# Turning keys and queries head by head into natural order, with one evacuation a bank

## The chip, the cores and the metric

One Trainium2 chip, one of its cores. The metric is the device time of one execution in microseconds (us), the median of several runs. Five engines work side by side, each through its own instruction list in order: TensorE (PE; its weight loads are shown as PEld), VectorE (DVE), ScalarE (ACT), GpSimd (POOL) and SyncE (SP), which issues nearly all DMAs.

## The reference, cut to what matters

Three stages in a row, on a batch of 2, 768 positions, 8 heads of 64 (512 channels):

```python
k_sum = k.reshape(B, H, nb, 32, D).max(axis=3)      # maxima of blocks of 32 keys
v_sum = v.reshape(B, H, nb, 32, D).mean(axis=3)
scores = concat([where(|i-j| < 16, q @ k.T / 8, -1e9), q @ k_sum.T / 8 + log(32)])
x  = softmax(scores) @ concat([v, v_sum])            # heads side by side: (2, 768, 512)
h  = relu(x @ w_in);  x2 = (h * sigmoid(conv3(h)) @ w_out)     # 512 -> 1024 -> 512
out = x2 + relu(layernorm(x2) * g @ w_ch1) @ w_ch2   # 512 -> 2048 -> 512
```

The weights come as float64 and are narrowed to float32 on the chip.

## The kernel before, in words

Work is cut into some 1,850 pieces ("ops" of a plan). Each has a name, the engines it may run on, and the pieces it must follow; the string ORDER lists all of them, each with the letter of the engine it runs on (P, V, A, G, S). The list is fixed in the file, and each engine's instructions stand in the order of the list. A piece that waits therefore holds up all later pieces of its engine.

**Attention.** The 1,536 positions are 6 chunks of 256 (0 to 2 are batch 0, 3 to 5 batch 1). Keys of a chunk become `kw`, queries `qb`: the 64 channels of a head lie on partitions, even heads on partitions 0 to 63, odd heads on 64 to 127, four heads each along the free axis, then positions. To get there, rows from HBM are turned by TensorE into a PSUM bank of 128x512 (`transposed`, L342, two banks a chunk; pieces `kt`, `kb`, `qt`) and the bank is evacuated to SBUF (`ke`, `kn`, `qe`). There are two layouts of a load. In a "pair" load (L324, keys 0 to 2 and all queries) a partition holds positions 2p and 2p+1 of every head, so that a piece of HBM is 512 B. A transposed bank then has the even positions on its lower 64 partitions and the odd ones on its upper 64, and the evacuation is two instructions of 64x512 that write every second position (L413, L801). In a natural load (L879, keys 3 to 5) a partition is one position, a piece of HBM is 256 B, two heads make one transposed block, and the evacuation is one instruction of 128x512 (L377). Block maxima (`km`, L810) are taken of `kw` for chunks 0 to 2, one instruction of 128x1024 a chunk, and of the bank (`kmb`, L369), one of 128x512 a bank, for 3 to 5. Copies of keys at the edges of 64-position windows (`kh`, `kx`) and of the maxima (`kc`) complete `kw`.

A pair of windows j (0 to 11) then goes: mask and scores on PE (`M`, `S`; L462, L470), maximum on DVE (`X`, L523), exponential on ACT (`E`, L535), sum and its inverse on DVE (`Q`, `R`), normalisation (`N`, L554, POOL or DVE), transpose on PE (`P`, L564), evacuation (`C`, ACT or DVE, tile probT), product with values (`T`, L486), and the split into a high and a low part (`H` on ACT or DVE, `L` on DVE, L508). Values come by `lv` (SP, L599, 256 B pieces); block means of values of batch 0 by matmuls on a pair load (`vb`, L826), of batch 1 by DVE reductions (`vr`, L944).

**Middle layers.** 48 steps i (6 chunks of positions by 8 blocks of 128 hidden channels): `h` (12 matmuls, L701), relu on ACT (L713), three taps (`b` on any engine; two DVE instructions, L729), tanh on ACT, gate on DVE (`g`, L742), high part on ACT (`u`, L753), low part on POOL (`v`, L760), and `x`, 2 x 3 matmuls into the output (L773). Weights come by `lw` into six staging places and are narrowed by DVE, ACT, DVE, ACT, POOL in turn (`wi`, `wo`: L621, L625, L630, L640, L642). The `wo` tiles lie where the early loads of keys, queries and values were, and wait for those to be turned.

**Last layers.** Per batch: layer-norm statistics, normalisation, 32 DVE block transposes in two halves (`lr`, L1076), scaled high and low parts (`la` ACT, `lz` DVE, L1085). Then 32 rounds of `ch` (two halves of 12 matmuls, L1106), high and low part (`ca` ACT, `cv` DVE), and `ac` (six of 3 matmuls, L1141). Their weights (`lwy`, pieces `y`) go the same way as `w`.

The lines at issue in the old turning and evacuation of queries are

```python
T.transpose(pt[:, i * 128:(i + 1) * 128], t[:, (2 * i + hf) * 128:(2 * i + hf + 1) * 128], ident)   # L353
for r in range(2):                                                                                  # L415
    scaled(e, qb[n % 2][s, :, :, r:64:2], pts[key][64 * r:64 * r + 64].rearrange(...), SCALE)
```

Of the kernel before, what the change touches and what calls it, by code (L numbers as in the profile page):

```python
# [3 lines left out]
2G 0V 8S 6V 12S 11S 13S 58S 1P 3G 175G 225G 4G 10S 49V 154G 50A 51V 5G 9S 64S 33P 31P 34A 76S 32V 26P 24P 27A 14S 7G  # L4
157P 35V 158P 43P 25A 36V 15S 59V 60A 28V 29G 16S 44A 18P 61V 20P 37V 19A 70S 41P 21V 52P 42A 17S 22V 23G 78A 77V
88S 62A 65V 56P 38A 79V 63G 54P 66A 30V 159P 82S 55A 45P 67V 155S 80A 57V 68A 81G 39A 46P 40A 160V 72A 69G 94S 167V
161A 71V 47P 73V 100S 168A 162V 163V 164V 53V 89V 178S 48A 165P 169V 170V 171G 181P 180P 166V 90A 182P 84A 156V 172P
74A 91V 179S 373S 173A 83V 75G 190V 92A 174P 377S 183V 85V 93G 184A 106S 95V 191A 200S 185V 186V 187V 101V 96A 207P
192V 193V 188P 176A 205S 194G 177V 208P 209P 86A 189A 97V 87G 195P 102A 210V 211A 206S 217V 229S 196V 212V 197P 218A
213V 103V 214G 198V 398S 230P 108A 231P 219V 232P 220V 107V 98A 221G 109V 104A 99G 222P 240V 215P 110A 233V 223A  # L10
199V 241A 105G 112S 201P 378V 111G 234A 118S 216V 124S 202A 399P 235V 236V 400P 374V 203P 237G 224P 393S 204A 421G
238P 242V 243V 375S 379S 226A 401P 244G 239V 227V 114A 422S 245P 113V 409V 246A 228V 120A 402V 250P 410A 119V 251P
115V 252P 121V 247P 116A 411V 412V 413V 253A 117G 254A 263P 248V 403A 394P 255V 264P 665G 130S 265P 256V 122A 423P
666S 424P 404V 266A 405V 425P 406V 123G 257A 267A 249V 126A 276P 426V 277P 395A 268V 278P 136S 269V 414P 258V 279A
407P 125V 259A 289P 127V 270A 260G 132A 290P 433V 291P 415A 131V 261P 292A 408V 293A 280G 262P 271V 427A 281V 302P
# [12 lines left out]
698V 517A 536P 677A 518G 720P 537A 505G 549P 728V 538G 550P 686G 539V 551P 525V 506P 540V 552A 526V 541A 685P 527V
721V 528A 740S 699P 687V 722A 562P 529V 507P 688V 530A 519P 723V 724V 542V 725V 520P 543A 531G 563P 564P 544G 532P
565A 566V 553G 533P 567V 568V 545P 554V 569A 546V 726P 575P 727A 555V 576P 700A 570V 577P 556A 547P 578A 557V 558A  # L30
706P 548V 571A 588P 559G 729A 1130V 589P 572G 560P 1128V 1129V 590P 730V 731V 707V 732G 561P 591A 1131V 592A 579V
741P 742P 593V 743P 580V 581V 601P 744V 582A 573P 751V 745A 602P 583V 603P 594V 712P 604A 746V 747V 733P 584A 748G
605V 614P 595A 752A 615P 585G 734V 574P 606V 616P 607V 869P 713V 608A 586P 617A 868P 587P 753V 754V 609V 870P 596V
755V 597A 610A 627P 598G 878V 735P 871V 611G 879A 890G 756P 749P 891S 757V 628P 872A 629P 880V 881V 882V 599P 630A
873V 874V 875V 892P 640P 631G 618A 619V 641P 642P 620V 632V 736G 893P 621A 600P 622V 643A 633V 612P 623A 737V 634A
624G 613P 738V 625P 644V 635V 708P 645V 636A 646V 637G 647A 750V 867S 626P 709A 648V 894P 710V 649A 650G 739V 758P
902V 895V 876P 759A 761P 877V 896A 762P 760V 763P 883P 764A 897V 898V 638P 899V 884A 765G 774P 903A 766V 775P 767V
776P 768A 639P 904V 905V 777A 906G 769V 778A 651P 653P 779V 652A 780V 770A 900P 654V 781A 907P 771G 901A 787P 1132V
908A 788P 1134V 789P 782V 772P 790A 1135V 1133V 1136V 783A 1137G 791V 800P 773P 801P 784G 792V 802P 785P 793V 803A
# [65 lines left out]
ALU = mybir.AluOpType  # L105
AX = mybir.AxisListType
# [54 lines left out]
def local_summary_attention_moe_kernel(  # L161
# [180 lines left out]
    def transposed(nm, n, hf, ring):  # L342
# [908 lines left out]
```

## Time and profile before

| | us |
|---|---|
| median of 3 runs | 510.57 (509.83 to 513.29) |
| the profiled execution | 509.58 |
| its span | 507.8 |
| PE busy in the span | 481.0 (95%) |
| DVE / ACT / POOL busy | 320.0 / 232.6 / 138.5 (63 / 46 / 27%) |
| mean granted TensorE clock | 0.99 |

The span is cut into 40 slices of 12.7 us on the profile's page; the attention and the narrowing of weights fill the first five, the middle layers run from about 50 to 240 us with the rest of the attention between them, and the last layers from about 212 us to the end.

### The profile page before, as it was taken

What the parts mean: (1) busy time and instruction counts of PE and PEld (TensorE: products, weight loads), DVE (VectorE), ACT (ScalarE), POOL (GpSimd) and SP (SyncE); (2) the same over time, 40 slices, a digit from 0 to 9 for tenths busy, and PEclk for the clock granted to TensorE, in tenths of its full rate; (3) what the DMA queues carried; (4) which work ended last, traced back from release to release, by engine and by line L of the source; (5) the groups of instructions that cost most, each with busy time, mean ns of one, the idle gap of its engine ahead of it and who ended that gap; (6) DMA issues with size and microseconds to landing.
All of it is one profiled execution on the core that took longest, in us unless ns stands there. A gap on an engine that the chain in (4) does not pass through costs nothing.

```text
span 507.8 us, 8440 instructions
## 1 busy us (share of the span) xinstructions
PE 481.0 (95%) x3222; PEld 414.9 (82%) x3222; DVE 320.0 (63%) x624; ACT 232.6 (46%) x607; POOL 138.5 (27%) x166
## 2 busy tenths in 40 slices
PE   6777899999999989999999999999999999999996
PEld 4355788888888877778898899988999899999995
DVE  4989899988897799999999933241443112221113
ACT  5988788776656565555554512242233011011110
POOL 4456455533323333315433201132224000000000
PEclk9889999999999999999999999999999999999999
DMA  8999957201020130002442500252220000200003
GB/s 271 344 260 277 197 143 170 70 1 33 18 45 1 38 131 0 1 1 85 163 159 92 166 1 1 83 166 83 84 83 1 0 1 1 105 21 1 0 1 125
DMA packets 56096, 43.44 MB, mean 86 GB/s; under 512 B 26092, under 2 KB 50952, under 8 KB 56056
## 3 DMA queue, kind: packets, MB, share of 16 engines
q1 hardware_dynamic: 55912, 42.78, 29.4%
q8 instruction: 25, 0.41, 0.4%
q14 instruction: 15, 0.12, 0.1%
q10 hardware_dynamic: 144, 0.13, 0.1%
HBM read 39.22 MB, written 3.15 MB: 83 GB/s over the span
## 4 chain that ended last, share of the span: by engine, by line
PE 64%; DVE 16%; issue 6%; DMA 5%; ACT 4%; POOL 2%; SPq 2%; DVEq 0%; POOLq 0%; ACTq 0%
PE acc L1141 22%; PE ch L1106 22%; PE h L701 7%; PE x L773 6%; DVE c L729 5%; DVE xf L1076 3%; POOL wl L642 2%; DMA raw<-in_moe_w_ch_dram 2%; PE sc L470 2%; DMA wst<-in_moe_w_out_dram 1%; DMA early<-in_q_dram 1%; DVE g L742 1%; PE tr L564 1%; PE av L486 1%; DVE parts L944 1%
## 5 line engine op out<-in xcount | busy, mean ns | idle before, releaser
L1141 PE MATMUL acc<-wh,ch 128*128 128x512 f32 x382 | 126.8, 395 | 0.7 <-DVE ch L1117 0.7
L1117 DVE SCALAR_TENSOR_TENSOR ch<-ch,ch 128x384 fp32r<-128x384 f32 x64 | 35.2, 555 | 127.9 <-ACT ch L1113 127.6
L1113 ACT ACTIVATE ch<-ch 128x384 fp32r<-128x384 f32 x64 | 30.9, 492 | 161.8 <-PE ch L1106 89.9
L1106 PE MATMUL ch<-xnT,wh 128*128 128x384 f32 x512 | 99.9, 337 | 0.0
L1106 PEld LDWEIGHTS ch<-xnT,wh 128*128 128x128 f32 x512 | 90.7, 188 | 4.7 <-DVE ch L1117 0.7
L701 PE MATMUL h<-xT,wi 128*128 128x258 f32 x576 | 83.8, 290 | 7.2 <-ACT h L713 6.9
L701 PEld LDWEIGHTS h<-xT,wi 128*128 128x128 f32 x576 | 74.8, 189 | 16.3 <-ACT h L713 12.3
L1141 PEld LDWEIGHTS acc<-wh,ch 128*128 128x128 f32 x382 | 71.5, 188 | 16.3 <-DVE ch L1117 1.5
L1141 PE MATMUL acc<-wl,ch 128*128 128x512 f32 x191 | 75.1, 393 | 0.0
L642 POOL TENSOR_TENSOR wl<-raw,wh 128x512 fp32r<-128x512 f32 x32 | 43.6, 1374 | 108.6 <-ACT wh L640 77.5
L760 POOL TENSOR_TENSOR glo<-g,ghi 128x256 fp32r<-128x256 f32 x48 | 39.9, 837 | 84.4 <-ACT ghi L753 77.5
L773 PE MATMUL x<-wo,ghi 128*128 128x512 f32 x192 | 61.6, 401 | 0.2 <-ACT ghi L753 0.2
L729 DVE SCALAR_TENSOR_TENSOR c<-h,ccol,c 128x256 f32<-128x256 f32 x96 | 53.5, 568 | 5.3 <-ACT c L251 3.2
L1106 PE MATMUL ch<-xnT,wl 128*128 128x384 f32 x256 | 54.9, 336 | 0.0
L1106 PEld LDWEIGHTS ch<-xnT,wl 128*128 128x128 f32 x256 | 45.4, 188 | 0.0
L1141 PEld LDWEIGHTS acc<-wl,ch 128*128 128x128 f32 x191 | 35.8, 188 | 6.6
L773 PE MATMUL x<-wo,glo 128*128 128x512 f32 x96 | 38.0, 396 | 0.1
L1076 DVE STREAM_TRANSPOSE xf<-xn 32x384 f32<-32x384 f32 x64 | 36.5, 570 | 1.4
L773 PEld LDWEIGHTS x<-wo,ghi 128*128 128x128 f32 x192 | 32.3, 189 | 4.7 <-ACT ghi L753 0.7
L535 ACT ACTIVATE prob<-sc,nm 128x120 f32<-128x120 f32 x96 | 33.2, 367 | 1.9 <-DVE nm L523 1.4
L734 ACT ACTIVATE c<-c 128x256 f32<-128x256 f32 x48 | 20.1, 419 | 23.5 <-DVE c L729 23.1
L640 ACT CAST wh<-raw 128x512 fp32r<-128x512 f32 x32 | 20.7, 659 | 14.8 <-DVE raw L630 12.6
(130 smaller groups left out, 584.0 us busy)
## 6 DMA issues: line engine op xcount, KB each, us to landing
raw<-in_moe_w_ch_dram SPq DMA_DIRECT2D x32, 512.0 KB, 5.2
wst<-in_moe_w_out_dram SPq DMA_DIRECT2D x8, 512.0 KB, 6.0
vw<-in_v_dram SPq DMA_DIRECT2D x20, 192.0 KB, 4.2
wst<-in_moe_w_in_dram SPq DMA_DIRECT2D x5, 512.0 KB, 7.9
s_q<-in_q_dram SPq DMA_DIRECT2D x4, 512.0 KB, 7.0
early<-in_k_dram SPq DMA_DIRECT2D x3, 512.0 KB, 5.1
x2a<-in_moe_w_in_dram SPq DMA_DIRECT2D x3, 512.0 KB
early<-in_v_dram SPq DMA_DIRECT2D x3, 512.0 KB, 7.2
```

Of the source, the lines that this page charges most:

```text
L535: A.activation(out=pr[:, p, :], in_=sc[:, p * NK:(p + 1) * NK], func=AF.Exp, bias=nm[:, p:p + 1], scale=1.0, accum_out=sm[:, p:p + 1])
L640: d = plan.op(name + "d", (("A", 520),), lambda e: A.copy(hi(), narrowed(raw())), [c_] + list(extra))
L642: lambda e: G.tensor_tensor(out=lo(), in0=narrowed(raw()), in1=hi().bitcast(F32), op=ALU.subtract),
L701: T.matmul(live["h", i][:, 0:CH + 2], w_[:, c, f * 128:(f + 1) * 128], x_[:, c, :], start=(k_ == 0 and c == 0), stop=(k_ == 2 and c == 3))
L729: V.scalar_tensor_tensor(out=ct, in0=ht[:, kk:kk + CH], scalar=ccol[:, kk * NF + f:kk * NF + f + 1], in1=ct, op0=ALU.mult, op1=ALU.add)
L760: on[e].tensor_tensor(out=glo, in0=live.pop(("g", i)), in1=live["ghi", i].bitcast(F32), op=ALU.subtract)
L773: T.matmul(x2ps[g, t], l[:, ts_], r[:, f, :], start=(f == 0 and j == 0), stop=(f == NF - 1 and j == 2))
L1076: V.transpose(out=o_, in_=i_)
L1106: T.matmul(cp[:, 0:384], w_[:, c * 128:(c + 1) * 128], x_[:, c, s], start=(n_ == 0), stop=(n_ == 11))
L1113: A.activation(out=chs[b, m][0][:, s], in_=live[key][:, 0:384], func=AF.Relu)
L1117: V.scalar_tensor_tensor(out=lo[:, s], in0=live.pop(key)[:, 0:384], scalar=0.0, in1=hi[:, s].bitcast(F32), op0=ALU.max, op1=ALU.subtract)
L1141: T.matmul(acc[key], l[:, ts_], r[:, 512:1024], start=(mm == 0 and j == 0), stop=(done and j == 2))
```

## The change

For keys 0 to 2 and queries 0 and 1 the load stays a pair load, but a bank is now made by eight plain matmuls instead of four transposes: the data (one head, one parity of positions: 128x64) is the stationary operand, the identity (128x128) the moving one, the result goes to 64 partitions and to every second column. Even heads land on the lower half and odd heads on the upper half, positions in natural order. Queries 2 to 5 get a natural load (two DMAs of 256 KB in 256 B pieces instead of one of 512 KB in 512 B pieces) and the four transposes that keys 3 to 5 had. All evacuations of keys and queries are one instruction of 128x512. Block maxima of keys 0 to 2 are read from the bank, six instructions of 128x512 instead of three of 128x1024.

```diff
-        if nm == "k" and n >= NCH:
+        if n >= (NCH if nm == "k" else 2):
             tv = t.rearrange("p (r h e) -> p r h e", h=4, r=2)
...
         else:
-            for i in range(4):
-                T.transpose(pt[:, i * 128:(i + 1) * 128], t[:, (2 * i + hf) * 128:(2 * i + hf + 1) * 128], ident)
+            tv = t.rearrange("p (h a e d) -> p h a e d", h=4, a=2, e=2)
+            ov = pt.rearrange("p (h j e) -> p h e j", h=2, e=2)
+            for i in range(2):
+                for e in range(2):
+                    for a in range(2):
+                        T.matmul(ov[64 * a:64 * a + 64, i, e, :], tv[:, 2 * hf + i, a, e, :], ident,
+                                 start=True, stop=True)
...
-                s = slice(64 * pp, 64 * pp + 64)
-                for r in range(2):
-                    scaled(e, qb[n % 2][s, :, :, r:64:2],
-                           pts[key][64 * r:64 * r + 64].rearrange("p (h w j) -> p h w j", h=4, w=NW), SCALE)
-            es = [plan.op(f"qe{n}{pp}", (("A", 956), ("V", 1196)), f,
+                scaled(e, qb[n % 2][:, 2 * pp:2 * pp + 2], pts[key].rearrange("p (h w j) -> p h w j", h=2, w=NW), SCALE)
+            es = [plan.op(f"qe{n}{pp}", EVAC, f,
...
-            e_ = plan.op(f"ke{n}{hh}", (("A", 956), ("V", 1196)), f, [t])
+            e_ = k_evac(n, hh, t, [])
+            KE[n].append(e_)
+            KM[n] = KM.get(n, []) + [kmax_op(n, hh, t, key)]
             e_.give.append((r_, key))
-            KE[n].append(e_)
+            KM[n][-1].give.append((r_, key))
...
+    def q_load(m):
+        b, c = divmod(m, NCH)
+        def f():
+            t = s_q()
+            tv = t.rearrange("p (r h d) -> p r h d", h=H, r=2)
+            for r in range(2):
+                t0 = c * CH + 128 * r
+                nc.sync.dma_start(out=tv[:, r], in_=q[b, :, t0:t0 + 128, :].rearrange("h p d -> p h d"))
...
```

The string ORDER is replaced as a whole. What is in it, by the names of the pieces:

- Engines. Of 24 `N`, POOL has 19 (10 before), DVE 5 (14). Of 24 `C`, ACT has 17 (13), DVE 7 (11). Of 12 `H`, ACT has 9 (7), DVE 3 (5). Of the 12 evacuations of queries, DVE has 5 (3), ACT 7 (9); of those of keys 0 to 2, DVE has 1 (2), ACT 5 (4). Two `xh` and one `kx` go from DVE to POOL; two `vs`, which were DMAs, and two `kc` go to DVE. Other moves are single ones. In all DVE has 594 pieces (609), ACT 431 (425), POOL 158 (144), SP 69 (71).
- SP, to the load of queries 3: before lc0 lk2 lk1 lq0 lw0 lk0 lc1 lw1 lw3 lq1 lvp0 lvp1 lw2 lvp2 lw5 lw4 lv0 lw6 lw7 lv1 vs1 lvb0 lvb2 lw8 lq2 lv2 vs2 lv3 lv4 lw9 lw10 lw11 lq3; after lc0 lw0 lk2 lw2 lk1 lk0 lw1 lq0 lw3 lw5 lq1 lc1 lvp0 lw6 lw4 lvp1 lw7 lvp2 lw8 lv0 lvb0 lvb2 lv1 lq2 vs1 lv2 lw9 lw10 lv3 lw11 lq3.
- PE, at the start: before the turning of queries 1 stands ahead of S0 and the three `vb` together behind it; after, S0 stands ahead of the turning of queries 1, and the `vb` are spread between S0 and S2. Around the first middle step: before ... P7 h0 T3 h1a qt30 ..., after ... P7 h0 M10 h1a h1b T3 M11 S5 h1c qt30 ... .
- Last layers of batch 0, second half: before, all its `lz` on DVE stand ahead of g47, the gate of the last middle step; after, ten of its sixteen `lr` and its four `lz` stand behind g47, and on PE six `ac` stand between the last `x` and the first `ch` that needs that half (ch011).

## Rows read from the trace of the kernel before

**Rows 1.** The span in 40 slices of 12.7 us: busy tenths of PE and DVE, granted TensorE clock in tenths, mean busy share of the DMA engines.
```profile
PE   6777899999999989999999999999999999999996
DVE  4989899988897799999999933241443112221113
PEclk9889999999999999999999999999999999999999
DMA  8999957201020130002442500252220000200003
```

**Rows 2.** Stretches (us, length; busy us and instructions of PE, PEld, DVE, ACT, POOL; granted clock; DMA busy share; GB/s).
```profile
20.00:40.00 20.00, 16.69 (x193) 9.79 (x191) 17.60 (x39) 17.83 (x65) 11.12 (x10) 0.83 1.14 273
40.00:60.00 20.00, 15.16 (x213) 12.19 (x206) 17.96 (x36) 16.74 (x54) 10.36 (x9) 1.00 1.13 259
...
120.00:140.00 20.00, 20.00 (x211) 17.21 (x210) 17.43 (x42) 13.51 (x58) 6.22 (x8) 1.00 0.06 13
```

**Rows 3.** The same columns for the stretch in which the middle layers end and the last ones begin.
```profile
165.00:185.00 20.00, 19.27 (x174) 16.81 (x174) 16.89 (x34) 10.75 (x28) 6.20 (x10) 1.00 0.31 107
185.00:205.00 20.00, 16.64 (x103) 14.01 (x102) 19.35 (x35) 12.33 (x29) 7.27 (x8) 1.00 0.00 0
205.00:232.00 27.00, 25.20 (x148) 21.44 (x147) 26.03 (x49) 13.59 (x34) 8.12 (x10) 1.00 0.01 2
```

**Rows 4.** What PE waited for between 165 and 285 us (total us, times, longest).
```profile
PE h L701 <- ACT h L713: 5.5, 6, 1.4
```

**Rows 5.** PE's timeline at the start (start us, us, in brackets the idle time before it and what ended it).
```profile
15.62 1.61 PE L353 MATMUL tr<-ident,early 128*128 128x128 f32 x8 [2.57 <-DMA early<-in_q_dram]
17.15 1.88 PE L470 MATMUL sc<-kw,qb 64*64 64x120 f32 x32
18.96 5.52 PE L826 MATMUL x<-early,ind 128*24 128x512 f32 x12
...
49.34 1.70 PE L701 MATMUL h<-xT,wi 128*128 128x258 f32 x12 [0.37 <-DVE xT L253]
...
54.72 0.63 PE L353 MATMUL tr<-ident,s_q 128*128 128x128 f32 x4 [1.54 <-DMA s_q<-in_q_dram]
```

**Rows 6.** The chain of waits, three pieces of it in order of time (start us, us): a bank of four transposes, one `x` of three matmuls, one `T`, all at full clock.
```profile
100.49 0.44 PE tr L353 x4
100.92 0.70 PE x L773 x3
...
113.51 1.08 PE av L486 x32
```

**Rows 7.** Groups of instructions, shapes apart (busy us, mean ns of one): evacuations of queries and keys, block maxima.
```profile
L251 ACT ACTIVATE qb<-tr 64x512 f32<-64x512 f32 x16 | 10.2, 640 | 0.9 <-PE sc L470 0.6
L255 DVE TENSOR_SCALAR qb<-tr 64x512 f32<-64x512 f32 x6 | 4.1, 689 | 0.1
L251 ACT COPY kw<-tr 64x512 f32<-64x512 f32 x4 | 2.5, 613 | 0.1
L251 ACT COPY kw<-tr 128x512 f32<-128x512 f32 x4 | 2.1, 591 | 0.1
L373 DVE TENSOR_REDUCE ksum<-tr 128x16 f32<-128x512 f32 x6 | 4.0, 682 | 0.1
L811 DVE TENSOR_REDUCE ksum<-kw 128x32 f32<-128x1024 f32 x3 | 3.7, 1220 | 0.2
```

**Rows 8.** The same view: pieces that change engine (`N`, `C`, `H`).
```profile
L554 POOL TENSOR_TENSOR prob<-prob,sm 128x480 f32<-128x480 f32 x10 | 10.4, 1044 | 16.2 <-DVE sm L547 7.5 <-ACT ghi L753 4.1 <-PE tr L564 2.1
L554 DVE TENSOR_TENSOR prob<-prob,sm 128x480 f32<-128x480 f32 x14 | 10.0, 713 | 0.4
L253 DVE COPY probT<-tr 120x512 f32<-120x512 f32 x11 | 7.5, 680 | 2.0 <-PE tr L564 2.0
L251 ACT COPY probT<-tr 120x512 f32<-120x512 f32 x13 | 7.4, 601 | 1.3 <-PE tr L564 1.2
L253 DVE CAST xT<-av 128x512 fp32r<-128x512 f32 x5 | 3.4, 686 | 0.6 <-PE av L486 0.6
```

**Rows 9.** The same view: the largest kinds of DVE work between 100 and 260 us, and two of POOL and ACT.
```profile
L729 DVE SCALAR_TENSOR_TENSOR c<-h,ccol,c 128x256 f32<-128x256 f32 x96 | 53.5, 568 | 5.3 <-ACT c L251 3.2 <-POOL c L255 0.6
L742 DVE SCALAR_TENSOR_TENSOR g<-c,h 128x256 f32<-128x256 f32 x48 | 21.1, 453 | 3.5 <-ACT c L734 3.0
L1076 DVE STREAM_TRANSPOSE xf<-xn 32x384 f32<-32x384 f32 x64 | 36.5, 570 | 1.4
L1085 DVE SCALAR_TENSOR_TENSOR xnT<-xf,ccol,xnT 128x384 fp32r<-128x384 f32 x16 | 10.1, 654 | 0.2
L760 POOL TENSOR_TENSOR glo<-g,ghi 128x256 fp32r<-128x256 f32 x48 | 39.9, 837 | 84.4 <-ACT ghi L753 77.5 <-PE tr L564 4.5 <-DVE xf L1076 2.4
L753 ACT CAST ghi<-g 128x256 fp32r<-128x256 f32 x48 | 19.0, 408 | 15.0 <-DVE g L742 8.0 <-PE x L773 6.4
L642 POOL TENSOR_TENSOR wo<-wst,wo 128x512 fp32r<-128x512 f32 x8 | 11.6, 1454 | 5.3 <-ACT wo L640 5.3
```

**Rows 10.** Transfers: two stretches (columns as in rows 2), the first with loads in 512 B pieces only, the second with keys in 256 B pieces; and the issue of the load of queries 3 on SP (start us, us).
```profile
6.00:9.00 3.00, 3.00 (x15) 2.73 (x13) 1.42 (x3) 1.91 (x4) 0.06 (x1) 1.00 1.13 363
80.20:82.00 1.80, 1.80 (x17) 1.75 (x16) 1.80 (x2) 1.44 (x5) 1.72 (x3) 1.00 1.22 218
...
45.20 0.38 SPq L330 DMA_DIRECT2D s_q<-in_q_dram x1
```

More of the change, by code (lines that the diff above doesn't have):

```diff
@@ new lines @@
+1053V 1063A 1017P 1030A 1040V 1054A 1173V 1019P 1031G 1041A 1018A 1170V 1073P 1020A 1074P 1042V 1055V 1075P 1043A
+1172V 1032P 1044G 1076A 1169V 1033P 1077G 1064A 1065V 1180A 1086P 1066V 1174A 1087P 1078V 1056A 1175V 1088P 1176A
+1057G 1045P 1182V 1178A 1067A 1046P 1089A 1179V 1090A 1058P 1329V 1091V 1099P 1177V 1059P 1092V 1100P 1079V 1093A
+1181V 1101P 1080A 1184V 1291P 1094V 1068V 1081V 1069A 1183V 1082A 1070G 1102A 1185V 1112P 1083G 1188V 1113P 1191V
+1114P 1285P 1187V 1115A 1192V 1116A 1103A 1194V 1104V 1071P 1117V 1286A 1105V 1292A 1072P 1287V 1106A 1118V 1095A
@@ L91 @@
+1763P 1755A 1756V 1774P 1773P 1772P 1764A 1766P 1765V 1781P 1767A 1782P 1768V 1785P 1784P 1794P 1783P 1786P 1798P
+1795P 1793P 1799P 1797P 1796P 1800A 1802P 1801V 1787P 1803A 1804V 1790P 1788A 1789V 1805P 1791A 1817P 1792V 1809P
+1808P 1821P 1811P 1807P 1819P 1810P 1822P 1820P 1806P 1818P 1812A 1814P 1813V 1829P 1815A 1823P 1816V 1834P 1824A
+1830P 1825V 1835V 1838P 1832P 1839V 1826P 1833P 1827A 1831P 1828V 1840P 1844P 1841V 1836P 1845V 1842P 1837V 1848P
+1843V 1846P 1849V 1847V
 """
@@ L800, in local_summary_attention_moe_kernel @@
             t = tr_op("k", n, hh, [lk[n]], ring=r_)
-            def f(e, n=n, hh=hh, key=key):
-                for r in range(2):
-                    scaled(e, kw[n][64 * hh:64 * hh + 64, :, :, K0 + r:K1:2],
-                           pts[key][64 * r:64 * r + 64].rearrange("p (h w i) -> p h w i", h=4, w=NW))
-            e_ = plan.op(f"ke{n}{hh}", (("A", 956), ("V", 1196)), f, [t])
+            e_ = k_evac(n, hh, t, [])
+            KE[n].append(e_)
+            KM[n] = KM.get(n, []) + [kmax_op(n, hh, t, key)]
             e_.give.append((r_, key))
-            KE[n].append(e_)
+            KM[n][-1].give.append((r_, key))
             early_reads.append(t)
-        def f(e, n=n):
-            V.tensor_reduce(out=ksum[0][:, :, 8 * n:8 * n + 8],
-                            in_=kw[n][:, :, :, K0:K1].rearrange("p h w (a t) -> p (h w) a t", t=32),
-                            op=ALU.max, axis=AX.X)
-        KM[n] = [plan.op(f"km{n}", (("V", 1135),), f, KE[n])]
         k_halo(n)
@@ L889, in k_load @@
         return dma(f"lkb{m}", 2912, f, after, take=[("s_k", ("k", m))])
+    def q_load(m):
[6 more added lines that the diff above has]
+                nc.sync.dma_start(out=tv[:, r], in_=q[b, :, t0:t0 + 128, :].rearrange("h p d -> p h d"))
+            stage["q", m] = t
+        return dma(f"lq{m}", 2912, f, take=[("s_q", m)])
     def k_keep(m, ld):
@@ L985, in local_summary_attention_moe_kernel @@
         if n >= 1 and n + 1 < NG:
-            for x in q_chunk(n + 1, dma(f"lq{n + 1}", 1456, load_pairs("q", q, *divmod(n + 1, NCH), s_q),
-                                        take=[("s_q", n + 1)])):
+            for x in q_chunk(n + 1, q_load(n + 1)):
                 x.give.append(("s_q", n + 1))
```

165 lines of the change are left out of this document (78 added, 87 removed).

## The prediction

> **What bounds the kernel now.** I read the 40 slices first [rows 1]. TensorE (PE) is below nine tenths only in the first five slices, in slice 15 (178 to 190 us) and in the last. After slice 19 (241 us) it is full to the end, and VectorE (DVE) mostly idle from slice 25 on: that half is a fixed amount of PE work, and the change touches nothing in it. So the change pays only where PE has gaps. Stretches of 20 us size them [rows 2]: from 20 to 60 us PE is idle for 3.3 + 4.8 = 8.1 us, and part of the rest runs at a clock of 0.83, while DVE and ACT are busy for about 88% and 86% and the DMA engines are full (share 1.13 to 1.14). From 120 to 140 us PE has no gap. From 165 to 232 us it is idle for 0.7 + 3.4 + 1.8 = 5.9 us, with DVE busy for 62.3 of 67 [rows 3]; what ends PE's idle time is almost always the relu on ACT (5.5 us in 6 waits [rows 4]), and that relu waits for a place in a ring that the DVE taps and gate free. So there DVE sets the pace. PE's timeline gives the start [rows 5]: it waits for the load of queries 1 until 15.62, then runs S0, then the three `vb` for 5.5 us, reaches the first middle step at 49.34 and waits 1.54 us for the load of queries 3 until 54.72.
>
> **The change part by part.**
>
> *Evacuations.* Before, six banks of keys and twelve of queries take two instructions each, 0.61 to 0.69 us apiece; one of 128x512 takes 0.59 on ACT [rows 7], about 0.69 on DVE. 18 x 0.6 = 11 us of ACT and DVE time go. Block maxima stay level: 3 x 1.22 = 3.7 against 6 x 0.68 = 4.1.
>
> *Other engines for pieces.* Nine `N` go from DVE to POOL: 9 x 0.71 = 6.4 us less on DVE, 9 x 1.04 = 9.4 more on POOL [rows 8]. Net four `C` and two `H` go to ACT: 4.1 us less on DVE, some 3.6 more on ACT. I summed the pieces of both lists with the means of their groups. DVE loses 13.5 us in all. Ahead of the first middle step 5.4 us less stand on DVE and 5.3 less on ACT; ahead of the gate of step 35 15.9 less on DVE, since some weight narrowing is also placed later.
>
> *PE.* Ten banks (six of keys 0 to 2, four of queries 0 and 1) take eight plain float32 matmuls instead of four transposes (0.44 us [rows 6]). No row has this form. The nearest is `T`: 32 plain float32 matmuls, 64 moving columns, 64-column weights for two halves of partitions, 1.08 us or 34 ns each [rows 6]; at 128 columns 67 ns, so 0.54 a bank. The other end is `vb`: 5.52/12 = 460 ns for 512 columns [rows 5], 115 for 128, so 0.92 a bank if the halves don't overlap. It can't be below the 0.44 of four transposes, because as many columns stream. I take 0.54: +0.1 x 10 = 1.0 us, upper end 4.8. The keys' six lie where PE waits for loads (2.57 us before 15.62 alone [rows 5]), so +0.4 counts. Writing every second column of a bank is in no row; I take it as free. For queries 2 to 5 PE's work is unchanged.
>
> A rule speaks against this step. The Trainium skill, "TensorE: Matmul & The Clock Gate", section Terms, says that transpose mode is four times faster for FP32, and plain matmuls don't use it; by that a bank would take some 1.8 us and the sum would be 13 us worse. The trace disagrees: `T` streams plain float32 at 67 ns per 128 columns of a half, not at four times a transpose's 110.
>
> *Loads.* Four loads of queries turn from 512 B into 256 B pieces. Full DMA engines moved 363 GB/s of the first and 218 of the second [rows 10]: 0.524 MB takes 2.4 instead of 1.44 us, +0.96 each. Queries 4 and 5 come when the DMA engines have room (slices 7 and 8 [rows 1]); without that they would cost those 2 us. Queries 2 and 3 come while the engines are full. Each load also issues once more on SP, 0.4 us [rows 10], ahead of value loads; SP has slack by then.
>
> *The start.* SP now sends weights 0 and 2 ahead of keys. At 1.44 us a load, and with queries 1 (eighth of the large loads) in at 15.6, the seventh, now queries 0, lands near 14.2. Two banks take 1.6 us as in [rows 5], one evacuation 0.7: S0 at 16.5 instead of 17.15, and the 5.5 us of `vb` no longer hold up S1. New waits: DVE narrows weights 2 and 1 between the block maxima, so kmb20, kmb11 and kmb10 stand behind the landings of weights 2 and 1 (third and sixth load: 8.4 and 12.7); the copies `kc`, and S0, wait for them until about 16, the same moment. A bank is freed by evacuation and maximum, not by evacuation alone, +0.7 us; the next user is a turning of keys, whose load lands later anyway.
>
> With 5.4 us less on DVE ahead of h0, h0 could start at 44 instead of 49.3, if DVE and ACT alone pace it; 0 is the other end, if transfers do. PE soon reaches the turning of queries 3, which waited for its load until 54.72. Counted in the list of SP, about as many bytes stand ahead of that load as before (one `lv` fewer, two loads at the slower rate), and the DMA engines are full; but its issue at 45.20 [rows 10] followed the turning of queries 2 out of the only buffer, and that comes 3 us earlier. I take 2.0 us gained, nearer the lower end, since the row that blocks is a transfer. PE has no gap afterwards, so it is kept.
>
> *The middle.* Of 5.9 us of idle time from 165 to 232 all could go, as 15.9 us less DVE work stand ahead. Late next is the second half of batch 0's norm: behind g47 DVE has ten `lr` and four `lz`, 5.7 + 2.6 = 8.3 us [rows 9], until ch011, while PE from g47 on has u and v to wait for (0.41 + 0.84 [rows 9]), two `x` at 0.70 [rows 6] and six `ac`, of as many matmuls of that size, 6.9 in all: 1.5 comes back. Gain 4.4, bounds 0 and 5.9.
>
> **Sum**: -2.0 - 4.4 + 0.4 = -6.0; 509.58 - 6.0 = 503.6 for a profiled execution. The profiled one lies 1.0 below the median of 510.57, so the median comes to 504.6; I say 504.5.
>
> **Rivals.**
> 1. *Covered gain.* Transfers pace the start, so that PE only waits longer for queries 3, and in the middle the late half of the norm, not the step's ring, becomes the wait. For it: full DMA engines until 60 us, the 1.54 us wait. Against: 62 of 67 us of DVE time is a tight bound, and 16 us of it leave. Start 0, middle -2.0, PE +0.4: 509.0.
> 2. *Slower: POOL.* Nine `N` move to an engine that takes 1.04 instead of 0.71 and whose list holds weight pieces of 1.45 us [rows 8, 9]. An `N` behind one is late by 0.33 + 1.45 = 1.8 us; `P`, `C` and `T` follow, and PE stands at `P` because its list is fixed. Nine times 1.8 is 16 us, 526 with no gain; only N0 and N2 lie before h0, +3.6, and the others stand among middle steps, so a half is more like it: 518. It decides where `N` ends later than PE reaches its `P`. Against: POOL is about half busy from 20 to 60 and a third later [rows 2].
> 3. *Plain float32 costs four transposes a column.* Ten banks at 4 x 0.44 = 1.8, +13 us, less 3 hidden behind loads, with the gains 514, without 520. This is the rule named above. `T` speaks against it.
> 4. *It doesn't reach PE at all*: the new list is no shorter in wall time, 510.6. I count it with the first.
>
> **Chances.** Forecast 0.52 (own range 500 to 505.4), first with fourth 0.33, POOL 0.11, plain float32 0.04. About 1% (5.1 us) is what a measurement of this kernel can tell: faster means below 505.5, slower above 515.7. Half of the third rival falls inside 1%, and so does a part of POOL. Faster 0.52, same 0.37, slower 0.11. Range: the low end is both gains nearly whole, 510.6 - 5.4 - 5.9 = 499.3, with 1.3 for more weight work moved; the high end takes in the covered gain and POOL's start. 498 to 513.
>
> **What would show it.** First middle step at 46 to 48 us; the turning of queries 3 still ended by its load, near 53; a bank of eight matmuls in 0.5 to 0.6 us at full clock; PE idle from 165 to 232 below 2.5 us, waits for the relu below 2; DVE busy near 307, ACT near 227, POOL near 149; a wait of 1 to 2 us at the first ch011. Wrong if: PE waits at `P` for POOL by several us, eight matmuls take over 1 us, or h0 starts at 49 or later.

## The result and the profile after

The kernel after takes 497.48 us (median of 4 runs, 494.84 to 500.24); the kernel before, beside it, 510.47 (509.83 to 513.29). The ratio is 0.9736, 95% interval 0.9672 to 0.98: 13.0 us faster. I had forecast 504.5 with a range of 498 to 513. The direction was right, the gain more than double the 6.0 of my sum, and the time lies 0.5 us below the low end. The profiled execution after took 497.72 us, 0.2 above its median, where that of before lay 0.9 to 1.0 below: from profile to profile the gain is 11.9 us, and one more of the 13.0 is only in which execution was profiled.

The page of the kernel after: busy time of each engine, then rows of the 40 slices (12.4 us each).

```profile
PE 478.9 (97%) x3342; PEld 417.3 (84%) x3342; DVE 306.5 (62%) x600; ACT 225.7 (46%) x601; POOL 149.6 (30%) x183
...
PE   6887999999999999999999999999999999999996
...
DVE  4998989877677898999999931251463011410114
...
PEclk9999999999999999999999999999999999999999
```

Against [rows 1], slice 15 of PE is full now, and the clock no longer dips in slices 2 and 3. The engines' busy times are those I had summed (307, 227, 149). The stretches of both kernels, in the columns of [rows 2]; first after, to 300 us:

```profile
0.00:20.00 20.00, 14.59 (x170) 11.06 (x171) 12.80 (x22) 11.46 (x20) 11.52 (x35) 1.00 0.94 290
20.00:40.00 20.00, 16.66 (x202) 9.22 (x203) 19.73 (x40) 17.78 (x66) 14.72 (x12) 1.00 1.14 270
40.00:60.00 20.00, 18.05 (x254) 15.34 (x252) 17.96 (x36) 17.05 (x67) 11.22 (x13) 1.00 1.15 259
60.00:97.00 37.00, 36.40 (x314) 31.58 (x313) 32.99 (x65) 27.04 (x69) 21.52 (x31) 1.00 0.76 146
...
165.00:232.00 67.00, 65.16 (x408) 56.27 (x407) 62.84 (x127) 43.92 (x102) 24.49 (x28) 1.00 0.19 64
232.00:300.00 68.00, 68.00 (x345) 61.56 (x344) 56.19 (x105) 25.27 (x48) 16.44 (x12) 1.00 0.28 93
```

and those of before that [rows 2, 3] don't hold:

```profile
0.00:20.00 20.00, 13.58 (x85) 9.01 (x86) 13.29 (x26) 14.33 (x24) 8.23 (x30) 0.91 0.96 302
...
60.00:97.00 37.00, 36.00 (x314) 31.43 (x312) 35.14 (x69) 30.68 (x80) 20.93 (x30) 1.00 0.54 129
...
232.00:300.00 68.00, 67.29 (x335) 59.52 (x334) 61.33 (x117) 32.41 (x60) 23.23 (x18) 1.00 0.38 124
```

PE's idle time falls by 1.0 + 0.0 + 2.9 + 0.4 = 4.3 us in the first 97 us, by 4.1 from 165 to 232 (5.9 to 1.8) and by 0.7 behind that, 9.1 in all. The rest is not idle time: before ran its 13.58 and 16.69 busy us to 40 us at a mean clock of 0.91 and 0.83, after at 1.00. Against that stands the extra work of the new banks. Busy time is partly modelled, so I sum no closer than this. This says where the time went and not why.

PE's timeline of the kernel after (start us, us, idle before):

```profile
13.46 1.95 PE L358 MATMUL tr<-ident,early 128*64 128x128 f32 x32
15.43 1.09 PE L358 MATMUL x<-ident,early 128*64 128x128 f32 x16
...
18.93 1.05 PE L473 MATMUL sc<-kw,qb 64*64 64x120 f32 x32 [1.19 <-ACT kw L252]
20.02 1.97 PE L358 MATMUL tr<-ident,early 128*64 128x128 f32 x32
...
47.50 1.72 PE L704 MATMUL h<-xT,wi 128*128 128x258 f32 x12
...
53.91 0.60 PE L351 MATMUL tr<-ident,s_q 128*128 128x128 f32 x4
```

The first middle step starts at 47.50 (49.34 before [rows 5]); the turning of queries 3 follows with no wait for its load, where 1.54 us stood before. S0 is later than before, not earlier: 18.93 against 17.15, behind an evacuation of keys. And a bank of eight plain matmuls is 16 instructions in the trace, two for each: two banks start 1.97 us apart (13.46 to 15.43), 0.99 a bank.

PE's waits over the whole span (total us, times, longest):

```profile
PE x L358 <- DMA early<-in_k_dram: 3.0, 1, 3.0
PE tr L567 <- POOL prob L557: 2.3, 3, 1.4
PE av L489 <- DVE parts L951: 1.4, 1, 1.4
...
PE h L704 <- ACT h L716: 1.1, 2, 0.9
```

The waits for the relu, 5.5 us between 165 and 285 us in [rows 4], are 1.1 in the whole span. A wait at the first product of the last layers that needs the second half of the norm, which I had expected, is not in the list. Three waits for POOL's `N` take 2.3 us.

The groups that answer to [rows 7, 8]:

```profile
L252 ACT ACTIVATE qb<-tr 128x512 f32<-128x512 f32 x7 | 4.2, 598 | 2.8 <-PE tr L351 1.6 <-PE sc L473 1.0 <-PE tr L358 0.2
L256 DVE TENSOR_SCALAR qb<-tr 128x512 f32<-128x512 f32 x4 | 2.7, 678 | 0.0
L557 POOL TENSOR_TENSOR prob<-prob,sm 128x480 f32<-128x480 f32 x19 | 20.3, 1068 | 18.2 <-DVE sm L550 14.6 <-PE sc L473 1.4 <-PE x L776 1.1
```

Each of these instructions costs within 3% what its counterpart in the trace of before had cost; what was mis-sized lies elsewhere.

### The profile page after: what moved, and what is told of

It is laid out like the page before. It is cut to its first block, busy times and chain, and to the rows that moved or that the text cites. A ratio compares the mean times of both kernels' runs of the same rounds, so it can differ in the third digit from the quotient of the medians.

```text
span 496.0 us, 8646 instructions
## 1 busy us (share of the span) xinstructions
PE 478.9 (97%) x3342; PEld 417.3 (84%) x3342; DVE 306.5 (62%) x600; ACT 225.7 (46%) x601; POOL 149.6 (30%) x183
## 4 chain that ended last, share of the span: by engine, by line
PE 81%; DVE 6%; DMA 6%; SPq 2%; ACT 2%; issue 1%; POOL 1%; DVEq 0%; ACTq 0%; POOLq 0%
PE ch L1112 27%; PE acc L1147 26%; PE h L704 10%; PE x L776 10%; PE av L489 2%; DMA s_k<-in_k_dram 2%; DVE c L732 2%; DMA vw<-in_v_dram 2%; PE sc L473 1%; PE tr L567 1%; DMA raw<-in_moe_w_ch_dram 1%; PE tr L351 1%; DMA early<-in_k_dram 1%; SPq L662 1%; DVE g L745 1%
## 5 line engine op out<-in xcount | busy, mean ns | idle before, releaser
L732 DVE SCALAR_TENSOR_TENSOR c<-h,ccol,c 128x256 f32<-128x256 f32 x96 | 51.2, 544 | 7.9 <-POOL c L256 4.6
L628 ACT ACTIVATE raw<-raw 128x512 f32<-128x512 f32 x32 | 20.6, 677 | 17.8 <-DMA raw<-in_moe_w_ch_dram 17.8
```

Source lines behind the costliest of these rows:

```text
L628: A.activation(out=f, in_=f, func=AF.Prelu, scale=F64_SCALE, alpha=F64_SIGN)
L732: V.scalar_tensor_tensor(out=ct, in0=ht[:, kk:kk + CH], scalar=ccol[:, kk * NF + f:kk * NF + f + 1], in1=ct, op0=ALU.mult, op1=ALU.add)
```

## The experiments

The theory at the start: DVE and ACT work saved ahead of the first step and of the middle gives the gain, through the code and through the engines in the list. The rival: the new list gives it, by the order in which pieces stand. A third: TensorE's clock, which falls at the start of the kernel before and not of the one after. Diffs that only change the list are given by what they put where; ratios are to the kernel before in the same series of runs.

**Code and list apart.**

```diff
-ORDER = list of after
+ORDER = list of before, ke -> kn, km n -> kmb n0, kmb n1
```

> The new turning, loads, evacuations and block maxima, with the pieces in the order and on the engines of the old list (the two block maxima of a chunk stand where its one maximum stood). Theory 'saved instructions': 11 us of DVE and ACT work are gone whatever the list, so most of the 13 us gain stays: 498 to 502. Theory 'list': the fixed order and the letters make the gain, the instructions only fill gaps: 507 to 511, PE idle from 165 to 232 us still about 5 us. Theory 'both': about half, 503 to 506.

511.24 us, ratio 1.0011 (0.9989 to 1.0034). The new code in the old list gives nothing. Its busy time falls on ACT (223.5 us, 232.6 before) and not on DVE (320.0 in both), the engine that I had called the pace. In its profile (513.22 us, the slowest of its runs) the start has become worse (first middle step at 52.77), and the gap of 165 to 232 stays at 5.1 us.

```profile
20.00:40.00 20.00, 15.49 (x159) 9.00 (x157) 15.77 (x33) 15.34 (x61) 9.31 (x8) 0.78 1.14 248
40.00:60.00 20.00, 14.81 (x180) 11.62 (x178) 18.18 (x34) 13.86 (x47) 11.06 (x10) 0.84 1.04 238
165.00:232.00 67.00, 61.94 (x432) 53.65 (x432) 59.83 (x112) 35.80 (x88) 20.45 (x26) 1.00 0.09 32
```

The other half, the code of before in the new list:

```diff
-ORDER = list of before
+ORDER = list of after, kn -> ke, kmb n0, kmb n1 -> km n
```

> The reverse: the old turning, loads, evacuations and maxima of the kernel before, in the order and on the engines of the new list (the one maximum of a chunk stands where its second bank's maximum stands). Theory 'saved instructions': 508 to 512. Theory 'list': 497 to 501. Theory 'both': 502 to 507, with the first middle step near 50 us as before and the idle time of PE from 165 to 232 us below 3 us, since the moved N, C and H still relieve DVE there.

500.72 us, ratio 0.9804 (0.9773 to 0.9835): 10 of the 13 us come with the list alone. DVE and ACT do 309.2 and 234.7 us of work, so ACT has even more than before, and the gap of 165 to 232 is 1.6 us. Its first middle step starts at 49.42, as in before. The code adds 3.2 us in that list, by medians of four runs each that leave about as much open; in the old list it adds nothing.

Could the slower loads of queries have eaten the saved instructions in the old list? e1 with the pair loads kept for all queries:

```diff
-            for x in q_chunk(n + 1, q_load(n + 1)):
+            for x in q_chunk(n + 1, dma(f"lq{n + 1}", 1456, load_pairs("q", q, *divmod(n + 1, NCH), s_q), ...
```

> The new code with the old list (511.2 us), but with queries 2 to 5 in pair loads and eight matmuls a bank, so that no load has 256 B pieces that had 512 B before. Theory 'the slower loads of queries ate the saved instructions in the old list': the waits for queries 2 and 3 shrink (1.7 us) and it becomes 507 to 509, in spite of 4 us more PE work. Theory 'nothing is saved where the list doesn't ask for it': 511 to 515.

512.87 us, ratio 1.0036 (1.002 to 1.0052), not better than e1. The loads are not what took the code's gain.

**Parts of the new code and list.** The same edit in the new list also tells PE's price of the eight-matmul form, since eight more banks use it:

> The changed kernel, with queries 2 to 5 loaded in pairs (one DMA of 512 KB in 512 B pieces) and turned by eight plain matmuls, as queries 0 and 1. Theory 'transfers pace the start': the two loads before 60 us are 0.96 us shorter each, up to 2 us faster, 495.5 to 497.5. Theory 'PE pays': eight more banks of eight matmuls at 0.5 us more each where PE is full, 4 us slower, 500 to 502.

501.79 us, ratio 0.984 (0.98 to 0.988), 4.3 us above after or 0.54 a bank, where four runs of each leave nearly 4 us open; PE's busy time rises from 478.9 to 482.8, 0.49 a bank. The group of the eight banks, in the kernel of this run:

```profile
L358 PE MATMUL tr<-ident,s_q 128*64 128x128 f32 x128 | 8.5, 277 | 0.0
```

128 instructions for 64 matmuls; 0.99 less the 0.44 of four transposes [rows 6] is 0.55, and the end of the kernel pays about that. That the second digits meet is luck.

Normalisations back on DVE (nine `N`: 0, 2, 8, 12, 14, 16, 19, 21, 22):

```diff
-N0:G N2:G N8:G N12:G ... N22:G
+N0:V N2:V N8:V N12:V ... N22:V
```

> The changed kernel, with only the nine moved normalisations N back on DVE, at the same places of the list. Theory 'DVE work ahead of the middle steps is what counts': 6.4 us more on DVE, PE idle between 160 and 230 us grows by 2 to 4 us, 499.5 to 502. Theory 'order alone': within 1.5 us of the changed kernel, 496 to 499. If POOL had been the new wait, it would become faster than 497.

498.13 us, ratio 0.9755 (0.9721 to 0.9789): 0.65 us above after, within what the runs can tell. DVE has 310.3 us instead of 306.5 at almost no cost, although the first middle step moves to 50.48 in this profile. So these runs show neither the rival "POOL" nor a gain from the nine moves.

All engines as before (evacuations of keys and queries apart), in the new order:

```diff
-letter of each piece as in after
+letter of each piece as in before, 68 pieces
```

> The changed kernel with its own order, but every piece back on the engine it had in the old list (the evacuations of queries and keys and the block maxima keep the new engine). With it DVE gets back some 13 us of work. Theory 'order of the pieces': 497 to 500, as the run with only N back. Theory 'relief of DVE': 503 to 508, PE idle from 165 to 232 us back to 4 us or more.

504.51 us, ratio 0.987 (0.9844 to 0.9896): 7 of 13 us are kept with the old engines. One row each of the clock and of the middle:

```profile
40.00:44.00 4.00, 3.38 (x36) 2.39 (x30) 4.00 (x7) 2.45 (x10) 3.25 (x3) 0.50 1.11 246
165.00:232.00 67.00, 65.28 (x445) 56.84 (x445) 60.70 (x122) 42.30 (x100) 24.98 (x32) 1.00 0.19 64
```

The middle's gap is closed (1.7 us) with the old engines. The converse, the new engines in the old order:

```diff
-order of after
+order of before, letters of after
```

> New code and new engines for all pieces, old order. DVE has the 13 us less work that the changed kernel has. Theory 'DVE's load decides': 500 to 504. Theory 'letters help only with the order that was made for them': 507 to 512.

521.32 us, ratio 1.0203 (1.0169 to 1.0237): 8.7 us less DVE work than before (311.3 us), and 10 us slower than before, 24 slower than after. A forecast from sums of engine time would have called this one a gain.

**Which stretch of the list.** New order up to the first middle step (h0), old behind it:

```diff
-[after to h0][after from h0]
+[after to h0][before from h0]
```

> New code; the pieces that the new list has ahead of the first middle step in the new order, all others in the old order and on the old engines. Theory 'the start and the middle add up': the start's 3 to 4 us of the 13 remain, 506 to 508, PE idle from 165 to 232 us about 5 us. Theory 'all is in the start': 497 to 501. Theory 'all is in the later order': 510 to 512.

510.72 us, ratio 0.9989 (0.9968 to 1.0009). The first step starts at 48.01, 1.3 us earlier than before, and nothing is left of it. Here is the wait that I had put into the forecast:

```profile
PE h L703 <- ACT h L715: 7.6, 9, 1.4
...
PE tr L350 <- DMA s_q<-in_q_dram: 3.1, 2, 2.6
```

The second line is the load of queries: my first rival, "covered gain", in a kernel that has only the new head. New order up to step 32, behind which the attention is done:

```diff
-[after to h32][after from h32]
+[after to h32][before from h32]
```

> New code; new order and engines up to the first matmul of middle step 32 (about 165 us), old order and engines for the rest. Theory 'the gaps from 165 us on close because less DVE work is left by then': 498 to 501, as the old order of the last stretch meets a DVE that is ahead. Theory 'the gaps close because of the order there': 504 to 507, PE idle from 165 to 232 us above 4 us.

503.69 us, ratio 0.9873 (0.9829 to 0.9917).

```profile
165.00:232.00 67.00, 61.11 (x384) 51.94 (x383) 62.81 (x115) 37.90 (x91) 23.46 (x28) 1.00 0.09 32
```

PE idles 5.9 us, as before, although this kernel has the new engines up to step 32. This is where my reason for the middle falls: the DVE work saved ahead of step 32 doesn't close the gap. Now the other way round:

```diff
-[before to h32][before from h32]
+[before to h32][after from h32]
```

> The reverse: new code; old order and engines up to middle step 32, new ones for the rest. Theory 'less DVE work left': 508 to 512, as DVE is behind when the new order begins. Theory 'order there': 502 to 505, the gaps from 165 to 232 us (here some us later) below 2 us.

507.01 us, ratio 0.9914 (0.9887 to 0.9942), 4.2 us below e1, and the gap is 2.0 us (e1 stands in another series of runs, whose before took 510.76 where that of e6 to e8 took 511.48):

```profile
165.00:232.00 67.00, 64.96 (x449) 56.45 (x448) 59.73 (x120) 43.12 (x103) 22.67 (x28) 1.00 0.19 64
```

Old work ahead of it, new order in it: closed. By the medians the list up to step 32, with the attention, is worth 7.5 to 9.5 us (e1 less e7, e8 less after), the last stretch 4.2 to 6.2 (e1 less e8, e7 less after). The profiles say where. PE's first product of step 32, in before and in after:

```profile
174.44 1.23 PE L701 MATMUL h<-xT,wi 128*128 128x258 f32 x8
```

```profile
168.87 1.23 PE L704 MATMUL h<-xT,wi 128*128 128x258 f32 x8
```

So 5.6 of the 11.8 us between the two spans are gained ahead of that point, though after still has one `x` of six matmuls (1.4 us) to run there that before has behind it. From that point to the end of the span it is 333.36 us in before and 327.13 in after, 6.2 less; in e1 and e7, with the old last stretch, it is 332.5 (from 179.01) and 332.3 (from 169.40), in e8, with the new one, 326.8 (from 177.92).

**What in the last stretch.** First tries: the second half of batch 0's norm moved behind the last gate, farther than after has it, in the list of e7.

```diff
-g39 ... lr01 x16 ... g43 lz013 ... lz012 lz011 lz010 ... g47
+g39 ... g43 ... g47 xn01 x3 lr01 x16 lz013 lz012 lz011 lz010
```

> New code, new order up to middle step 32, old order for the rest, as in the run with the old tail (503.7 us, PE idle 5.9 us from 165 to 232 us), but with one thing of the new tail: the second half of batch 0's norm (its normalisations, lr, la and lz) stands behind g47, the two first ch of that half behind the last x and six ac. Theory 'the old tail put norm work ahead of the steps on DVE, and the steps starve PE': most of the 6 us come back, 498 to 500.5, idle time from 165 to 232 us under 3 us. Theory 'the gaps have another place in the order': 503 to 505, idle still 5 us or more.

530.28 us, ratio 1.0379 (1.0335 to 1.0423). The edit had a fault of its own, which one line names:

```profile
PE x L775 <- ACT ghi L755: 11.8, 1, 11.8
```

ACT's share of the norm (`la01`) stood ahead of the last gate's high part (u47), and waited there for DVE. With those four behind it, six of the sixteen transposes ahead of the last gates, and one evacuation (`xe10`) on ACT instead of DVE:

```diff
-u46 t47 la013 la011 la010 la012 u47
+u46 t47 u47 ... la013 la011 la010 la012
...
-g44 ... g47 xn01 x3 lr01 x16
+g44 xn01 x3 lr01 x6 ... g47 lr01 x10
```

> The run with the old tail (503.7 us) again, with the second half of batch 0's norm late as in the new list, now without the fault of the first try, in which the scaling on ACT stood ahead of the high parts of the last steps: six of its sixteen lr stand behind g44, ten behind g47, its scaling on ACT behind xe11, six ac ahead of its first ch, and xe10 goes to ACT. Theory 'norm work ahead of the steps on DVE starves PE': 498 to 501, PE idle from 165 to 232 us under 3.5 us, fewer lr on DVE before 205 us. Theory 'the gaps have another place': 503 to 506, idle 5 us or more.

518.7 us, ratio 1.0145 (1.0114 to 1.0177), 15 us above e7. PE's waits from 232 to 262 us:

```profile
PE ch L1111 <- ACT wh L642: 4.7, 1, 4.7
PE ch L1111 <- DVE xnT L1090: 1.8, 1, 1.8
```

The late norm now holds up the last layers and, on ACT, the narrowing of their weights; and from 165 to 200 us, where its DVE list is still that of before, PE still waits 3.3 us for the relu (3.2 in before). Neither theory had this time, and the run doesn't show the cause; but the gap stands although the second half has moved. DVE's timeline of the kernel before in the gap shows another candidate:

```profile
190.75 1.15 DVE L1076 STREAM_TRANSPOSE xf<-xn 32x384 f32<-32x384 f32 x2
191.93 1.29 DVE L729 SCALAR_TENSOR_TENSOR c<-h,ccol,c 128x256 f32<-128x256 f32 x1
193.25 1.15 DVE L1076 STREAM_TRANSPOSE xf<-xn 32x384 f32<-32x384 f32 x2
```

Two block transposes of the *first* half (`lr00`) stand between one tap and the next. In the list of before, ten of the sixteen lie between the gates of steps 33 and 38 and its first product, ch010, stands within the `h` of step 43; in that of after five, with ch010 behind the `h` of step 46. So I took the kernel after and put the last twelve back there on DVE, and nothing else:

```diff
 g33 c34y
+lr00 lr00 (y10c) c34z lr00 lr00 c35y c35z
 g34
+lr00 lr00 c36y c36z lr00 lr00 (y11c) g35 lr00 g36 c37y lr00 c38y lr00 lr00
...
-lr00 x12 spread from c35z to g42
```

> The kernel after, with one thing moved: on VectorE the last twelve block transposes of batch 0's first half stand two a step between the taps of steps 34 to 38, as in the list before, instead of up to the gate of step 42. All other lists and all engines stay. Ahead of the gate of step 36 stand eight more of them, 8 x 0.57 = 4.6 us. Theory (PE idles between 165 and 232 us in the kernel before because these transposes crowd the taps of steps 33 to 38, so the relu's place in the ring comes free late): PE idle in that stretch goes from 1.8 us to 4 to 5.5, waits for the relu from 1.1 to 3 or more, ScalarE's waits for the taps from 3.5 to about 8, time 499.5 to 502. Rival (the place of the transposes on VectorE is not what counts, it is the order on TensorE and ScalarE, with the first product of the last layers behind step 46 instead of step 42): PE idle below 2.8 us, time within 1 us of 497.5.

503.08 us, ratio 0.9857 (0.9826 to 0.9888), 5.6 us above after, of which the runs leave some 3.5 open. The profiled execution, its fastest (500.46):

```profile
165.00:185.00 20.00, 20.00 (x146) 17.17 (x145) 18.73 (x38) 14.09 (x32) 8.74 (x11) 1.00 0.30 106
185.00:205.00 20.00, 16.38 (x101) 13.21 (x100) 17.52 (x34) 11.44 (x27) 5.80 (x7) 1.00 0.32 106
205.00:232.00 27.00, 26.13 (x143) 22.54 (x142) 23.72 (x49) 15.20 (x37) 8.08 (x11) 1.00 0.00 1
```

and two of its waits in that stretch, then the first of them in before:

```profile
ACT c L736 <- DVE c L731: 6.4, 6, 1.9
...
PE h L703 <- ACT h L715: 3.3, 4, 1.2
```

```profile
ACT c L734 <- DVE c L729: 14.8, 14, 2.6
```

The gap is back in its old place, 185 to 205 us: 3.6 us there (3.4 in [rows 3]), 4.5 in the stretch against 1.8 in after. The tanh on ACT waits longer for the taps (6.4 against 3.5 in after), the relu queues behind it in ACT's list, and PE waits for the relu. The theory expected 499.5 to 502 and waits of 3 or more; PE's waits agree, the time is 1 us over, and ACT's waits for the taps are 6.4 where about 8 were expected. Behind the first product of step 32 (at 167.62) this profile has 331.1 us, 4.0 more than after with the same PE list. So twelve transposes of 0.57 us, in another place of one engine's list, cost about 4 us, 5.6 by the medians. They are not the whole of before: there ACT waits 14.8 us for the taps, with ten of them in this place.

**The start.** SP's early loads in the order of after, everything else as in e1:

```diff
-SP: lc0 lk2 lk1 lq0 lw0 lk0 lc1 ...
+SP: lc0 lw0 lk2 lw2 lk1 lk0 lw1 lq0 ...
```

> New code, old order and engines, but SP's loads of the attention and of the first weights in the new order. Theory 'the order of the loads made the start': the start gains 3 us or more over the new code with the old list (511.2), 506 to 509. Theory 'no single engine's order does it': 510 to 516, as the other engines still ask in the old order.

528.63 us, ratio 1.0351 (1.0319 to 1.0384).

```profile
PE av L488 <- DMA vw<-in_v_dram: 7.8, 2, 7.5
...
PE x L820 <- DMA early<-in_v_dram: 5.4, 1, 5.4
```

Values now come later than the old PE list wants them. The order of loads is no gain by itself either.

The clock: the kernel before, with 20 more matmuls of zeros in four places of PE's idle time at the start, whose result nobody reads.

```diff
+    for i_, n_ in enumerate((9, 4, 4, 3)):
+        w_ = plan.op(f"wf{i_}", (("P", 210 * n_),), filler(n_), [w0_], take=[("h", f"wf{i_}")])
```

> The kernel before, with 20 extra matmuls of zeros (bf16, 128x512, into a bank that is free then) where PE waits at the start: nine ahead of the turning of queries 1, four ahead of the masks of pair 2, four ahead of the second P of pair 1, three ahead of T1. They only keep PE busy. Theory 'the start was slow because PE's granted clock fell to half after its waits (0.58 from 16 to 20 us, 0.5 to 0.6 from 32 to 40)': the clock stays at 1.0 and the first middle step comes 2 to 3 us earlier, 507 to 509. Theory 'DVE, ACT and transfers pace the start': no gain, 510 to 512.

511.9 us, ratio 1.000 (0.9976 to 1.0024).

```profile
32.00:40.00 8.00, 6.21 (x111) 4.18 (x112) 6.11 (x15) 5.06 (x21) 4.93 (x4) 1.00 1.12 234
44.00:48.00 4.00, 2.92 (x23) 1.77 (x23) 3.87 (x5) 3.61 (x15) 2.31 (x3) 0.50 1.23 230
```

The clock stands at 1.00 where it was low, and S3 starts at 38.30 (38.40 before): up to there the low clock doesn't set the pace. The run is no clean test behind that point, since the clock falls at 44 us instead, and the first middle step comes at 52.40, 3 us later than in before. The time is the same. In the new list e3 helps: its clock is 0.91 from 20 to 60 us, where after has 1.00, and its median is 0.65 us above after. So no run here shows the clock as a cause of the gain.

Last, the one wait of PE for DVE in after that looked as if it could be had: the block means of values `vr0` and `vr2`, ahead of which T1 waits 1.4 us, moved behind the pieces that T1 needs.

```diff
-X4 vr0 Q5 ... X6 vr2 C4
+L0 vr0 R4 ... L1 vr2 qe20
```

> The changed kernel with two of the four DVE reductions of values (vr0, vr2, 2 us each) behind the low part L0 and L1 that free the bank of T1 and T2; T1 waits 1.4 us on DVE there. Theory 'waits of PE at the start reach the end': 1 us faster, 496 to 497. Theory 'the start is paced by more than one engine': no change, 497 to 498.5.

498.2 us, ratio 0.9754 (0.9727 to 0.9781): no gain over after. The first middle step starts at 51.26 here, 3.8 us later than in after. Of its profile:

```profile
PE tr L566 <- POOL prob L556: 4.3, 4, 2.2
```

The wait for `vr` is gone and POOL's `N` ends last in its place (2.3 us in after, 4.3 here).

## Why the prediction was wrong, and what of it was right

The forecast from profile to profile was -6.0, the measurement -11.9. Both of its gains came out larger: ahead of step 32 the sum had -1.6 and the profiles have -4.2 to -5.6, behind it -4.4 against -6.2 to -7.6, by the side to which the one `x` is counted.

**The start: -2.0 forecast, about -4.3 of idle time measured, 4.2 to 5.6 us of time up to step 32, and 7.5 to 9.5 by the spliced lists.** The step that failed is "I take 2.0 us gained, nearer the lower end, since the row that blocks is a transfer". The transfer does block (2.6 us in one wait of e6), but only where the old list follows; in after its turning needs no wait, as PE has other pieces ahead of it. I had costed S0 and h0, two points of the list, and counted the gain at h0 as kept. The first step came at 47.50, inside my 46 to 48, but that was no support: e2, e3 and e14 start it at 49.42, 50.48 and 51.26 and are still 10 us or more faster than before, and e6 starts it at 48.01 and gains nothing. What I had not priced is what PE does in the waits between: from 40 to 60 us it is idle 1.95 instead of 4.84 us. Nor did I see that S0 at 16.5 would not come: it is at 18.93, and that costs nothing visible. The upper bound that I wrote down for the start, 5.4 from engine sums, was nearer; but e11 shows that such a sum is no reason. Which pieces of the new order carry the gain up to step 32 no run here separates; that cause stays open.

**The middle: -4.4 forecast (5.9 less 1.5 back), 4.1 in the stretch and 0.7 behind it; by the spliced lists 4.2 to 6.2, by the profiles 6.2 to 7.6 behind step 32.** The time gained was larger by 2 to 3 us. The idle time was about right, but the reason was wrong, so that this match is luck. "As 15.9 us less DVE work stand ahead": with the new list up to step 32 the gap stays whole (e7), with the old one it closes (e8). What counts here is the work that stands between the taps of steps 33 to 38, and e16 shows a large part of it: twelve block transposes put back there bring back 2.7 of the 4.1 us of idle time, and 4.0 us behind step 32 where e7, with the whole old last stretch and one `x` less to run, has 5.2. That the first half's products come three steps later in after gives room to spread them; this is read from the two lists, and I have not tried it alone. The 1.5 us that I had given back at ch011 did not appear; the last `x` and six `ac` stood ahead of it on PE, and that was enough.

**PE: +0.4 forecast.** My 0.54 for a bank of eight was a half: I had taken the 32 rows of `T` in the trace for 32 matmuls, and they are two rows for each. So 67 ns are for 64 columns, not 128. Measured 0.99, above the upper end that I had kept (0.92, from `vb`); ten banks are +5.5 us of PE work instead of 1.0, and my upper end was 4.8. What the ten cost in the end was not tried; the cover that I named, the waits for loads before 16 us, can hide a part, and two banks of queries 1 lie behind it (at 20 us). Where PE is full, the end pays about 0.5 a bank (e4). On the third rival: the Trainium skill, "TensorE: Matmul & The Clock Gate", section Terms, has transpose mode four times faster for FP32. The trace doesn't show that: a bank takes 0.99 us against 0.44, a factor of 2.2, and the eight matmuls stream 1,024 columns where four transposes stream 512, so that a column takes 0.97 ns against 0.86. My row against the rule was misread; the rival fails all the same, and what I had wrong is that the halves overlap.

**Loads and evacuations.** The evacuations cost what I took (0.60 on ACT, 0.68 on DVE). The slower loads of queries are not felt: with pair loads e4 and e15 are not faster than the kernels they are compared with, though both also carry more PE work (3.9 and 1.9 us in the profiles), which can hide a gain.

**The rivals.** Covered gain is what e6 shows, with a part of the change; the whole change escapes it. POOL: three waits, 2.3 us, and e3 within 0.65 us of after. "No shorter in wall time" fell with the result.

**The range.** My low end was both gains nearly whole. It had no place for what the new order gains between h0 and step 32, nor for more than the idle time behind it, and I carried the 1.0 us between profile and median over to the kernel after, where it is 0.2 the other way. Profile against profile the forecast was 503.6 and the measurement 497.72.

## What to carry to other kernels

Where each engine works through a fixed list, as here, a sum of saved engine time is no forecast by itself (e1, e11): ask which piece lies between two links of the chain that PE waits for, not how much work lies ahead. The code, the engines and the order of a plan belong together: the new list kept 10 of the 13 us without the new code (e2), while other parts, taken alone, gave nothing (e1, e6) or lost up to 18 us (e12). And before a duration is divided by a count of rows, count the instructions that one call in the code makes in the trace.

## What was not expected of the hardware

A plain float32 matmul with 128 moving columns shows as two instructions; eight of them for half the partitions each take 0.95 to 0.99 us at full clock in a row of two banks, and 1.02 as a single bank in e4; four float32 transposes of 128x128 take 0.44. By the column that is 0.97 and 0.86 ns: filling two halves of the partitions in turn did not shorten it. The granted clock of the kernel before falls to about half of full speed (1.2 of 2.4 GHz) at the start, and in the kernel after it does not; in before one such fall follows the stretch from 28 to 32 us, in which PE was busy for 1.70 of 4.00, where after was busy throughout. The rows of before, then of after:

```profile
28.00:32.00 4.00, 1.70 (x33) 1.29 (x30) 3.90 (x9) 3.76 (x19) 2.21 (x2) 1.00 1.21 241
32.00:36.00 4.00, 3.41 (x49) 2.28 (x49) 3.21 (x6) 3.57 (x13) 2.69 (x2) 0.63 1.02 218
36.00:40.00 4.00, 4.00 (x62) 3.00 (x58) 3.19 (x8) 3.11 (x11) 2.51 (x3) 0.52 1.21 259
```

```profile
28.00:32.00 4.00, 4.00 (x31) 1.70 (x34) 3.91 (x6) 4.00 (x19) 3.24 (x3) 1.00 1.20 249
```
